# Nine warm-up products on fewer rows, and ten unread operations on GpSimd, in a two-layer attention kernel

## The chip, the cores and the metric

The kernel runs on one core of one Trainium2 chip. The metric is the time of the program on the device in microseconds (us), the median of its runs. The core has a matrix engine (TensorE, PE in the profile, with its weight loads as PEld), VectorE (DVE), ScalarE (ACT), GpSimd (POOL) and SyncE (SP), which here issues most of the transfers. Each engine works through its own queue in order and waits on semaphores for the others.

## The reference

The input x is 2048 tokens of 512 features. Four blocks follow each other, A, B, A, B, each with a layer norm ahead of it and a residual sum behind it:

```
x = x + A(layernorm(x));  x = x + B(layernorm(x));  and both again
A: q, k, v = x@wq, x@wk, x@wv; 32 heads of 16; 4 segments of 512 tokens
   a_dot = softmax(q k^T / 4 + causal mask) v      inside the segment
   a_mem = phi(q) M / (phi(q) z + 1e-6)             memory of the segments before
   out = (g a_mem + (1 - g) a_dot) @ wo,  g = sigmoid(beta)
B: phi(t) = [softmax(t w_phi), softmax(-t w_phi)];  linear attention over all
   2048 tokens: (phi(q) (phi(k)^T v)) / (phi(q) sum phi(k) + 1e-6) @ wo
```

The layer norm needs, for each token, 1/sqrt(variance + 1e-5).

## The kernel before

Tokens lie on 128 partitions, 16 tiles of 128 tokens. A segment is four tiles. The program is written as a list of operations (`Graph.op`) with what each reads and writes. A table named ORDER, a packed text at the end of the file, says in which sequence they are put, which engine takes each (where more than one could), and which buffer each tile of data gets. `place` unpacks it and `emit` derives the waits. So the place of an operation in the source says nothing on when it runs: only the table does.

The parts that matter here lie in the first 25 us:

- `setup` issues the loads of x and of the weights, and makes the constants. `onesb` is a 128x128 tile of ones (L513). The gate is made from beta: an exp on ScalarE, an add (L517) and a reciprocal (L518) on VectorE, and with it each of four slices of the weights WA_v is scaled (L526). The table puts these four scalings on GpSimd; they are called the gates here. The V product of the first segment reads them.
- `ln` is the layer norm of a tile: statistics on VectorE (L570, L571), then for most tiles an add of epsilon (L578) and a power with exponent -1/2 (L580) on GpSimd, each of one column, and then the normalizing on VectorE (L591), which is transposed. The four tiles of the first segment take ScalarE for the root instead (L574, L576).
- `warm` gives PE products of ones with ones that nothing reads, while the first loads are under way. It has 26 units of one 128x512 product each, and after the fourteenth four extra units with small or half-height products. 25 of the 26, with the extras, stand ahead of the first segment's products in PE's queue; the transposes of the first four tiles stand between them.
- `a_proj` makes keys and queries of a segment, four groups of eight heads at a time (L341), evacuates them on ScalarE or VectorE (L359, L360), and multiplies the keys with masks that pick heads (L672). The scores are products of those (L326); their exps are on ScalarE (L351).
- `b_keys` and `kv_add` sum the keys-times-values of block B in the float32 tile KV32 (L890 the first of a layer, L892 the others).

GpSimd's queue at the place of the change is, in the table's order: the add and the power of one tile of the second segment (L578, L580), two gates (L526), two adds, a power, an add, two powers (L578, L580), a memset (L534), two gates, a memset, and further adds, powers and memsets. VectorE's queue there is: statistics of the next tiles, the gate's add and reciprocal between them, then masked key products and the normalizing of the second segment's tiles in alternation.

Of the kernel before, what the change touches and what calls it, by code (L numbers as in the profile page):

```python
# [1108 lines left out]
c-rlH1&|~;lC4}WR%KRIS2Hs+Gcz+YGcz+YGcz+YGcz+YbALs3&(7@b>@C>8|IN-WvQiOJgj~;`yT4SXRYFppR3H^e9HK}90t87VQkhgCRY^5cozx&TNi9;F)FE|AJ  # L1109
yM@EAPq?)(wH<MO-VD-oJ1i}Ni-6d#3ZqZCWKHTh$V(d;v<ZNBb?+S1xaR7h~y?&NC}dMWF>h?VG@s&B>6}-QiLQXrATR#pJXRRNf}ar<RC3bPSTPTBV|b|(waOY@y  # L1110
T<Ngp?ym$pdnQ+#(N26dIjeCAUc|`huh<k;zL^oJ=Pp$qX`z%p^<5Xfln=BNIq!l8W3R*T`M+h|DIhNL2cmTqm>0Tyl@hA!ErHa)b0HZAc%|mo$ZDFo?7zN8uQ>BQs
zogrg(K05XuorcX$F(vNf?{Yfv<g`^`XNeYsYM5Ad)9GaG_B*$SD*$5|K6ZlC02_pB&YjTr3B}>U+I0DPaIMR)bC-cc_5}T|cacKq;oh~4q$wU&KE+n1E3bLGZB_m)
0ydfiDBGiYsqy#j8lE7du{2=ehB+{KMB8v%!$poMy5fB7JNFdoq){zjhmh2~c$X-HVAABb3VFP4=DWoW5g{fpW`9QLRg<vQK*<dqS3R_4IQW};)8Q4lnfr6eSkQRc%
P!-BTLpVUHK_e&v#bFSX#hQ4KRE7*dp%xA%6`&l1077{fN-Dx&r~)-1BZPr?G!tZoWTZIypcYhz=Fk{wzyN3g1ECevhFQ=AhLM&~2WCS(7y`pd4EmLn!=X?Y){`Lmg
|vpYFbX!1jie2<gYp<mYhwf&k%pl=VKnT5BV-I5C6Q=Yh);9CSQrk&U<%BElQ0#=!zq{x@nI5-gUPTT4nP9f4bx#7Y=-$T5B5MfD1q-uauNWQ@f-O>4ERCAN3xS7gy
fJ2Qo|xx3=$T=LP!irASR7W!;?zT9wLyOumx5_8dw9#AUte^ZEy%Wz*yQ5VnGB5p@9&VMugZ96_P>}NCBOp6QqS+5Er^YSBL|VVLOQgy&)Y$gKkg~yF&#WN0-A2*bZ
l4C7gy;(2usD$LS8}PfySxbSP~}Khm}EogRdB@QMDQt!W=9g>|qm#DglB9(q6`5*^M$D|#OK!6tGJF2HvZi7bJhkdgL>U~&<Tk;(Kp$wYh8DYOsWMF!F)^bm;w+ek&
sOEc4^bPzpEn$avYCv8qsLN=P8=Aij#H`<*B;C}iDeAt5?pagqTz{k*+4yMEC0J?+pq9f^WI*QiC5wrjuO;bTVJVj!{C74NH!V`E6&tMk43{z<?m`2Cb+^~>dfvb=Q
uEB0Po9?04VFF!5=hFmq4qZT>)2B2ct%^6`CcL1}=pA?pci|Q!qG{+oxDVCv0VJns=@?oGZ^J`aOefMM^d+4~FOV7Z4O}Fz=p;Iw9;9>WV`}gaT~5=}6?7?GMsv~UP
#ss&SMUPf!YUe;L?kE42~q>w(%du;Jx$)h6Kav+dpJq=QjVwSC)h`i($8>=7NQgjQ$oK0BBkHpBYc1&v>+`<v(vngj+Uh5>0x?=uBNA{!ZlRmTDp!_q+4k*S{k>}ua  # L1120
K2ipvCESnuM;W8)yldl<uHA=|;MVrl6H5(9N_A`Y{mC(lhiN4aWEM0}VonZ|OUFkqZ1wFVQdbI(<!V(5v(teM4{3uk;!Xi(xPWElNW$9PXl9Xd8NqR;K4^6?%c@gFT
oZuF%``GObVdI_QaMRayXQ(FU{{tw~GM@4)CM{EYQ+8*ax2*bo!q9U6xv!jv=>txcO@4O*Svrw`~|nvDK{=2(X|r1$7UT9?LUoCY#M6JrWYim5P&eZY@68H3pr48s(
abSh56L#XLtoQH-k!TGop1L$&Gfj+tr8_`m<47D@~HbOsbfsN@RT!stq2(H9rY%%`8qc|RuGr~6D1l)+La1E};g0L1-;v}4i;jtbqOH<Pb_=wKLS-1mt;%wZ6?Pz<t
8RuXJIv11SK7547a6fLr<M<d;v3uAO@8fRVib>c(Jb=3}HG6<b*+XoNukbatL10br6viMYup>Q*t?)Fi!%lbxlVe+KjO+0%PREG&1u5%{UojFQV=M(r$s%JE?1Hf|D
h|dc$eCa-@F~8;A=rsN!_M>#e#hrH3P<Bx9Eu~b3r&q3uqnpDxEKwiV>}FDkyr%w4!_}h49g<3i0mB3W9Kmn8;-+JvoR={Vll8QwnxLp;sv~jX)r$Cz>XLbZ(=u$&!
VxYEIR9s8(A#Y12?hQEG>({(xQ*0Vg0Z_`dLrBgb7$W9LN%~TX-A$;z%5bm$47tLCdb-RZNe)Far)^G1)m1j<sj!Nn$pcbzq6uNfw?BW>eTHHiQkpLD&w*VQ=h8Gq7
uzj%6b0Sw@zL&A?a~h9tndm=O=NBP<iPVwtfu%ZhE-8Pb-GWdZCuW@cweUd(~xST1bGhO<sAANF7)SZCIgWy7491#@E_%#Qi702W~#Sr^uo6=l6xH<pEUXIWV>R+^P
yWm#|5m-S)&*m|~s6~w8m5EjO4EIXUVHnS~kJe$FWvSDl_o4`h~v+OjR#HO<|>>NAFMzbO~h8<%ESy7zGwz5NP8_U6RvV1H*E5~xN+$;|(&I+)CtPq>Yis39ao0Vj9
SYB3`?Phz}Ubd5MXUEwCwu9|r!1po9DOda<JJ0sB3+w<p!K$zyjPR<gKP$t^v$?Dk8^GqVi|i7+%&xGj>>B&VDzGQ4BCE}+vG43Do6qX7>Z}s0%$~8jtOk3|7O+R`I
{U(Iu*d8xTgVo%#q1`##g?$!tR7p*ma;qSE?dU#vHR>L)7<b^%yQ%boO8inum<b{^Yhp2BYVT%vWDy(d(V9Q5@Gx^`@}AjlzbIi&g!$8tQK3%*08l~1#8S2v30BoOU  # L1130
0YAKpxD)@E{(-!}8QT4G+iD^7K3%&%m3pm^?g>#WV5<JONL{Gx5wkHjm5S@#gG3Ps&@cWIQ2{$RqJMJTi~R6Z0rMDv!pq@RlqIkI$p?6g)Zqz(4ZpJO<Chi}1WWA1}
a*@*2DtugPoi$~-^M%CqsDJUh?D3-Us|FfYza@Eklhufj|6a=a8T&tLJ^yehB8OY;i65--au@-qAlugB}~y1X{8&l~U-Jd1qGTk?jy5pT?!@TR;OZ_Zoswmhr+#6R<
|yc_?*+wt!F8_y=c^X#%UZ_nHC4!k2DD|+*Bq7VPU-F8b*5mrnTJvfSRf{F2>Cyyi|i%FudBfA$5FCvI2q7(1OJM#%*vX~<J^Qc0I0bGi%ybB-0hj1mV2oMALU_OWs
<zu-PJ~4&Q;eL@pZV(yeMlp^L<Ky{oK9^76Q~3x!k5A+Cc|;LSWRg?G3^83y6Vb(15kt%rvqWaOO-$so#YjF!EZ}p+JTaZm;5p?YkwfN^x#cKsM4*T%7K>P7CSS-$^
I3cmpTuYLJaWFsD;M(xVlvMsQ;Pg@p(r2=$_ye%EEg+8u&6Ch^HTB*4-sKRA`x4x6strbSw|L@rR7<Eop0nt<tDz5@8`wjW`2q9<vaLgo=Pkc7x)1lM<f<Y#ZG>nXB
1oc7QT&d=Sf6Tv5Q~i$wX=qSHu%(L?)406p_hAT5*aW<xBVlxs(fahp!gP#6>ApWqFq`<5gr`d5&-3^<;dJKpf}0`8}RRWEIQ#8orXR;D`7szDXSBH+U{}pReXO`5u
`{<yLFNUU{3RRw+b6af>UpR>V<S#Z|pU0+mo@6ZK^ukxrx+>%|eiS*#NWc^TPP^b<Q}1G!%|lqu9Mc|c}S{Y6TZRh^Qj<p6O{R+ZaDBUw%E5XI$MK1d7{5BUSWMO2q
N#eKO??v{t-L77R#Q-|ddSwdu1@l|*gL6sCiY8^i+j`5@NxI7`t$`bOJyuwR~Dq^3gA+O1rvX(r-ON(H2U6vPB#V&D2UXpj^Ww~42kT>N6`B0vbXJtt_M6BoKWDi+E
R21dJ9<g5>6MMx~>9!#1mi#Wy%iHpbJSX$0A2P3stj>tb;<z{<PKZk4k$fV1%E$7Gcq+@wD2k{G(x^lVlvRmUb`eoUQdjv|(NUHWC&fW=Ra_IjWN%qXR+J~@NuE#T5
KQG)g+*g|N;Hwx#UB1lK9|?{X;E3^6xT(5QBB+sc|{G;Np_Z9WFC=A<QDlv5#d*X>V@Pgj0#ZE)GPT?77){vPn8viL_yI?9u^;EG4Wc4sAMXvN~5N$v?{r3CBmr;s<  # L1140
n8=qpIh;n~14i@K5rMEF^A<jH;$+Bf5)@qJXL;3aUrEuzJkTiSweVY$iX;w=$NxAUcTXs<mt<-pTj!i)<s?$`3Mzsx6v|W}<=kDw~TI;t7Asdx++;zGx^qiHoAB=p#
R<^s12hsIsY{0`xGEUG)@=#BkAB)DvAqW6@W(6m3O&QC!p&BSbIplGhR6<PmX6bQOa|6A@btQB>zp-_%g`U8PgQRZ?|9)l?(YMRiQoQpZ(Jl|;Q3C)69!K-E@_R9$s
a6;nl2aaB~6P&ZV6bxYh-1Jp>dLX8r)MML#gd>1X`5AjKi7IoAe@kKON&%|djR;^T{R7o{XT~nphXmwrP7iH94QCd}2WmP#9PcBmN<wNmYELL;WTs2T7kO}1&l}L_M
!_;`SL?xC>RT5c6)l(DHL^Vmh6O&a{RbC~PGt^AAOf6UQ)Dbmbtx~I11@%ExR7ce*HA{u)L29;ItE#E$s)-t`rl`~EmRhL7>f368dZgB<d#b5=tnRCDx|w>Q!s~~sz
FMaqiw)|d*r;BL^=gx9p_;39vWBXplF7|#s%j}8iLSDn{3>1ukVHNa?PYiQUUZP(L_e8aJ{5P=S#?fbQcu+rbzWUo!TPRxr&_8o`n}Tns%oXKs55GdGP;9mtvac;%5
A0eRuw@%5HHj-^-?`oW5jl~O|?<4RA;wwji}$Ku=1_?q<*My^0Ok^YLrql8K9L8FFUH3GEnYN?G%?g)hiK6Mv<}PJrPH8{Z);YJ{=^-NTL1O$Q1I6I;d01NIFRGQ<3
F<l}a8^yVOCoTTPOa<yd)0N0d@VkW=Iy6<bc%{pAc@RR`(;vaOD+m9+AZiYnvEVX~TTr-#e+a=$*HH^?YDnvSZY>w$8j+$3Y@FjC84IYMrfLe|sG^=4ULx6nQH7Fk3
0(lvEgRa@85>-7fRO)b=m^j0}l2FMV(O}1BER1Y;s4wl{3P?=gDR(n-U{aU5copoy6MaR+=bQ+ybXVevSW*u8^)IHTo-AirKt8`o)NBd-N)j*%t)pdJ)M)y%2^k!XG
Z_$->Uv*Jm(zSF~omR)wNpwHeP&d{?WFtLJHqqVmOx;O$)U$MD-BNegt#lQgRF9O&baI_S$Jg`q0^LLR)_wGHJyp-vt#v=$Mz7F^bzeP4Ptyr>Lfu~v)C2S&9Ze3_<
7FnDNH^8#^%1>TZ`IrMUOi7Q(fjmeeMK*p$Mp%lM6T9r^eVYpE|t+`7QI%Ek{R?0Iae>$%k*`9Ro~Fp^mN(Ev^MMXT76s3kazVReNS)KJM|8|OYe}|<q(}%r_?c|Up  # L1150
CY8<a{|(&XLRIN;yr=mJ{S|y+$sRx%5e$Tc6dZ^f{eJ7u5N5VSP)dkvDZ(nNIG}vt(X9SLWC2<WPNI57Q6zd3`~T(8KitSwt7m<MjlcUS`#W^aK4!r!=Wd8S_{l(?!
feQ`ThDMa?3U!#vSPbxzaE^fuXbGLzgq*H85e{Y)>EIrK}NQ;*c?O=^?DywYh*T9d-$GwDn*Gt*==`Asoh+{`kiOlh-7j?zW-L_JAQ)}!?poyBA_SxshBT$j`(bOF=
# [60 lines left out]
```

## Time and profile before

| what | us |
|---|---|
| median of two runs | 493.31 |
| lowest, highest | 492.28, 494.34 |
| the profiled execution | 492.6 |
| its span, first to last instruction | 490.9 |
| PE busy | 460.2 |
| VectorE busy | 436.1 |
| ScalarE busy | 433.9 |
| GpSimd busy | 59.6 |

Busy times overlap; each is the time in which the engine had an instruction running. In the views below, a row of a timeline gives start, length, engine, line and operation, what it wrote and read, and in brackets the idle time ahead of it with what ended it. A row of the groups gives the shape, the count, the busy time and the mean of one in ns. L numbers are lines of the kernel.

### The profile page before, as it was taken

The numbers are of one execution on the slowest core, as the hardware profiler recorded it, in microseconds if no ns is written. First come the engines' busy times: TensorE is split into PE (matmuls) and PEld (weight loads), VectorE is DVE, ScalarE is ACT, GpSimd is POOL, SyncE is SP. The second block draws the span as 40 slices with busy tenths as digits, with TensorE's granted clock in tenths as the row PEclk, the third lists the DMA queues.
The fourth block names the chain that finished last, engine by engine and source line by source line (L and its number), as shares of the span: only waits on it lengthen the run. The fifth ranks groups of instructions, "written<-read, shape, count | busy, mean of one in ns | idle before, by whom it ended". The sixth has DMA issues, their size and how long they took to land.

```text
span 490.9 us, 27235 instructions
## 1 busy us (share of the span) xinstructions
PE 460.2 (94%) x12490; PEld 309.1 (63%) x12490; DVE 436.1 (89%) x1087; ACT 433.9 (88%) x605; POOL 59.6 (12%) x144
## 2 busy tenths in 40 slices
...
POOL 4701031010011001000230240100010010100000
...
DMA packets 89459, 30.50 MB, mean 62 GB/s; under 512 B 76000, under 2 KB 89344, under 8 KB 89344
## 3 DMA queue, kind: packets, MB, share of 16 engines
...
q14 instruction: 17, 0.14, 0.1%
q0 software_dynamic: 64, 0.02, 0.1%
...
## 4 chain that ended last, share of the span: by engine, by line
PE 59%; ACT 25%; DVE 8%; issue 3%; DMA 3%; SPq 1%; POOL 0%; POOLq 0%; DVEq 0%
PE D L341 36%; PE D L326 21%; ACT p L351 16%; ACT pE L351 6%; DMA WA_q<-in_A_wq_dram 2%; DVE pQ L672 1%; ACT pS L351 1%; DVE p L756 1%; DVE pS L925 1%; PE D L854 1%; DVE pK L360 1%; ACT pV L359 1%; DVE p L591 1%; ACT p L359 1%; DVE p L360 1%
## 5 line engine op out<-in xcount | busy, mean ns | idle before, releaser
L351 ACT ACTIVATE p<-D 128x1024 bf16<-128x1024 f32 (+1 forms) x368 | 312.1, 913 | 25.2 <-PE D L326 11.6
L326 PE MATMUL D<-pK,pQ 64*128 64x128 bf16 (+1 forms) x2560 | 115.5, 211 | 4.3 <-ACT p L351 1.4
L326 PEld LDWEIGHTS D<-pK,pQ 64*128 64x128 bf16 x2560 | 80.7, 94 | 43.4 <-ACT p L351 10.9
L351 ACT ACTIVATE pE<-D 128x768 bf16<-128x768 f32 x128 | 102.0, 835 | 4.7 <-PE D L326 3.6
L326 PE MATMUL D<-pV,p 64*128 64x34 bf16 x1536 | 73.4, 176 | 3.9 <-issue 2.9
L326 PE MATMUL D<-pV,pE 64*128 64x34 bf16 x1024 | 75.2, 175 | 0.5 <-ACT pE L351 0.2
L326 PE MATMUL D<-pW,pE 64*128 64x34 bf16 x1024 | 73.0, 175 | 0.1
L326 PE MATMUL D<-pW,p 64*128 64x34 bf16 x1536 | 71.7, 176 | 1.0 <-issue 0.9
L326 PEld LDWEIGHTS D<-pV,p 64*128 64x128 bf16 x1536 | 66.8, 93 | 7.1 <-issue 2.4
L326 PEld LDWEIGHTS D<-pW,p 64*128 64x128 bf16 x1536 | 65.8, 93 | 3.9 <-issue 1.4
L341 PE MATMUL D<-pX,WA_k 64*128 64x512 bf16 x256 | 65.2, 376 | 2.1 <-DMA WA_q<-in_A_wq_dram 1.4
L341 PE MATMUL D<-pX,WA_q 64*128 64x512 bf16 x256 | 65.3, 377 | 0.6 <-issue 0.4
L578 POOL TENSOR_SCALAR rstd<-mv 128x1 f32<-128x1 f32 x60 | 14.9, 265 | 374.0 <-DVE mv L571 367.2
L326 PEld LDWEIGHTS D<-pV,pE 64*128 64x128 bf16 x1024 | 54.8, 93 | 3.1 <-issue 1.5
L326 PEld LDWEIGHTS D<-pW,pE 64*128 64x128 bf16 x1024 | 51.2, 93 | 0.9 <-issue 0.3
L570 DVE BATCH_NORM_STATS2 stats<-X 128x6 f32<-128x512 bf16 x64 | 42.5, 681 | 4.7 <-DMA X<-in_A_x_dram 4.6
L925 DVE TENSOR_REDUCE pS<-p 128x32 f32<-128x512 bf16 x64 | 42.1, 672 | 2.1 <-ACT p L351 1.9
L672 DVE TENSOR_SCALAR pQ<-p,m 128x512 bf16<-128x512 bf16 x128 | 42.6, 355 | 0.6 <-ACT p L359 0.5
L879 DVE TENSOR_TENSOR X<-X,D 128x512 bf16<-128x512 bf16 x48 | 31.1, 682 | 7.3 <-PE D L341 7.1
L580 POOL TENSOR_TENSOR rstd<-rstd,mhalf 128x1 f32<-128x1 f32 x60 | 36.4, 624 | 2.8
L341 PE MATMUL D<-WA_o,p 64*128 64x512 bf16 (+1 forms) x288 | 33.8, 353 | 2.3 <-issue 1.9
L326 PE MATMUL D<-tri,two 64*128 64x256 bf16 x256 | 35.2, 270 | 0.0
...
## 6 DMA issues: line engine op xcount, KB each, us to landing
...
p<-p SPq DMA_TRANSPOSE x76, 3.2
pX<-p SPq DMA_TRANSPOSE x54, 3.2
...
```

The lines of the kernel that those rows point to most:

```text
L326: ins = e.matmul(out_ap, lhsT, rhs, start=st, stop=sp, tile_position=(basep(lhsT), basep(out_ap)))
L341: ins = e.matmul(out_ap, lhsT[64 * hf:64 * hf + 64], rhs[64 * hf:64 * hf + 64], start=k == 0 and i == 0, stop=k == 1 and i == len(lists[hf ...
L351: return self.g.op({"act": (dur, lambda e: e.activation(out_ap(), in_ap(), func, scale=scale))}, reads, writes, opens, label=label)
L359: ch = {"act": (n / 1.2 + 51, lambda e: e.activation(out_ap(), in_ap(), ACT.Copy)), "dve": ((340 if fast else n / 0.96 + 65), lambda e: e. ...
L360: "dve": ((340 if fast else n / 0.96 + 65), lambda e: e.tensor_copy(out_ap(), in_ap()))}
L570: v(lambda e: e.bn_stats(self.stats[:, t, :], self.X[:, t, :]), 602, [R("X", t)], [R("st", t)], label="bn")
L578: v(lambda e: e.tensor_scalar(rs, self.mv[:, t, 1:2], LN_EPS, None, op0=ALU.add), 170, [R("mv", t)], [R("rstd", t)], eng="pool", label="rstd")
L580: v(lambda e: e.tensor_tensor(rs, rs, self.mhalf[:], ALU.pow), 540, [R("rstd", t), R("mhalf")], [R("rstd", t)], eng="pool", label="rstd")
L591: v(lambda e: e.tensor_scalar(xn.t[:], self.X[:, t, :], self.mv[:, t, 0:1], self.rstd[:, t:t + 1], op0=ALU.subtract, op1=ALU.mult), 300, [ ...
L672: fn = lambda e, KM=KM, KT=KT, sl=sl: e.tensor_scalar(KM.t[:, :, sl % 2, :, 64 * (sl // 2):64 * (sl // 2) + 64], KT.t[:].rearrange("p (j h ...
L879: self.v(lambda e, X=X, src=src: e.tensor_tensor(X(), X(), src(), ALU.add), 602, [R("X", t), ps[512 * k]], [R("X", t)], label="res")
L925: fn = lambda e, sgn=sgn, E=E, Z=Z: e.tensor_reduce(Z.t[:, sgn * 32:(sgn + 1) * 32], E.t[:, sgn * 512:(sgn + 1) * 512].rearrange("p (h d) ...
```

## The change

Two operations are added to `setup`: memsets of parts of KV32, used as scratch, on VectorE. Ten operations are added at the end of `build`, all for GpSimd (two rounds of five): a power of 128x64 float32, a power of 128x16, a product of 128x64, a product of a 128x256 bf16 tile with 2.0, and a sum of two such tiles. Nothing reads what they write. All KVacc sums are made to depend on the ten.

Nine of the 26 warm-up units become products on 64 or 32 rows, of 256 columns, two rounds over the row groups; those on 32 rows write into two PSUM buffers. The four extra units shrink.

The table is a new one. Unpacked, it differs from the old one as follows. GpSimd: the ten operations stand together behind the power of the last tile of the second segment (the L580 at 10.97 us in the profile) and ahead of the first two gates; nothing else differs. VectorE: the copy of L535 goes from far behind to third place; the two memsets stand among the first segment's normalizing and evacuations; the gate's add and reciprocal (L517, L518) go behind the next eight statistics operations (five L570, three L571) and the mask sum of L499. ScalarE: the exp of beta goes four places back. PE and SP have the same order. No operation changes its engine. Buffers of PSUM get other numbers, and two buffers of the pool p1 are exchanged in places.

```
+        flat = self.KV32[:].rearrange("p a b -> p (a b)")
+        self.probe, self.z64, self.pb = flat[:, 0:128], flat[:, 0:64], flat[:, 128:384].bitcast(BF16)
+        v(lambda e: e.memset(self.z64[:], 2.0), 70, [], [R("z64")])
+        v(lambda e: e.memset(self.pb[:, 0:256], 2.0), 100, [], [R("pb")])
...
-        D = self.T(self.pD, "S")
+        D, D2 = self.T(self.pD, "S"), self.T(self.pD, "S")
...
-                        ins = e.matmul(D.t[c0:, r0 * 8:r0 * 8 + n], r[:, c0:], ones(r, n), start=True, stop=True, tile_position=(r0, c0))
+                        ins = e.matmul((D if r0 < 64 or rows == 64 else D2).t[c0:, r0 % (rows * 2) * (512 // rows):r0 % (rows * 2) * (512 // rows) + n], r[:, c0:], ones(r, n), start=True, stop=True, tile_position=(r0, c0))
...
+        shapes = {14: 64, 15: 32, 16: 64, 17: 32, 18: 32, 19: 64, 20: 32, 22: 32, 23: 64}
         for k in range(N_WARM):
-            unit(128, 512, 1)
+            if k in shapes:
+                unit(shapes[k], 256, 2)
+            else:
+                unit(128, 512, 1)
             if k == N_WARM // 2:
-                for rows, n, m in ((64, 51, 12), (64, 64, 8), (64, 256, 4), (128, 34, 8)):
+                for rows, n, m in ((64, 51, 1), (64, 64, 1), (64, 256, 2), (128, 34, 1)):
                     unit(rows, n, m)
...
+        pr, one, v = self.probe, self.ones8, self.v
+        for r in range(2):
+            v(lambda e: e.tensor_tensor(pr[:, 64:128], self.z64[:], self.mhalf[:].to_broadcast([128, 64]), ALU.pow), 600, [R("z64"), R("mhalf")], [R("pr")], eng="pool", label="prb")
+            v(lambda e: e.tensor_tensor(pr[:, 64:80], self.z64[:, 0:16], self.mhalf[:].to_broadcast([128, 16]), ALU.pow), 600, [R("z64"), R("mhalf")], [R("pr")], eng="pool", label="prb")
+            v(lambda e: e.tensor_tensor(pr[:, 64:128], self.z64[:], self.z64[:], ALU.mult), 600, [R("z64")], [R("pr")], eng="pool", label="prb")
+            v(lambda e: e.tensor_scalar(self.pb[:, 256:512], self.pb[:, 0:256], 2.0, None, op0=ALU.mult), 600, [R("pb")], [R("pb2")], eng="pool", label="prb")
+            v(lambda e: e.tensor_tensor(self.pb[:, 256:512], self.pb[:, 0:256], self.pb[:, 0:256], ALU.add), 600, [R("pb")], [R("pb2")], eng="pool", label="prb")
+        for o in self.g.ops:
+            if o.label == "KVacc":
+                o.deps.update(self.g.ops[-10:])
```

More of the change, by code (lines that the diff above doesn't have):

```diff
@@ L641, in fn @@
                         r = self.onesb[r0:r0 + rows, :]
-                        ins = e.matmul(D.t[c0:, r0 * 8:r0 * 8 + n], r[:, c0:], ones(r, n), start=True, stop=True, tile_position=(r0, c0))
+                        ins = e.matmul((D if r0 < 64 or rows == 64 else D2).t[c0:, r0 % (rows * 2) * (512 // rows):r0 % (rows * 2) * (512 // rows) + n], r[:, c0:], ones(r, n), start=True, stop=True, tile_position=(r0, c0))
                 return ins
-            self.g.op({"pe": (m * max(n / 2.4 + 2.5, 26.0), fn)}, [self.R("onesb")], [D], label="warm", rows=rows if c0 == 0 else rows * 10)
+            self.g.op({"pe": (m * max(n / 2.4 + 2.5, 26.0), fn)}, [self.R("onesb")], [D, D2] if rows == 32 else [D], label="warm", rows=rows if c0 == 0 else rows * 10)
+        shapes = {14: 64, 15: 32, 16: 64, 17: 32, 18: 32, 19: 64, 20: 32, 22: 32, 23: 64}
         for k in range(N_WARM):
-            unit(128, 512, 1)
+            if k in shapes:
+                unit(shapes[k], 256, 2)
+            else:
+                unit(128, 512, 1)
             if k == N_WARM // 2:
-                for rows, n, m in ((64, 51, 12), (64, 64, 8), (64, 256, 4), (128, 34, 8)):
+                for rows, n, m in ((64, 51, 1), (64, 64, 1), (64, 256, 2), (128, 34, 1)):
                     unit(rows, n, m)
@@ L1108 @@
 ORDER = """
[L1109 to L1152, printed above, removed]
@@ L1153 @@
-Cyw(LxOOwmwHgEJ>{Z5b7@AX&xL4VUz^f+C}bTXYyVYA+pH|0!8lhBkfc})_t!6Y(?O;XdrbToNPAJf+iFau2~J;apOL(O;nQGe1u^k-ec5L3xiG?h&moy}A+Uo@CO
-ri&@7+nB+ot7&V>X==*r?53*eVbJt6&CGDq-h?sDjW*UWBg|^E#)Oz|rkZJIwwg#LiV17Nn{CDzZlnn?KBG)^Q^V9W{mn45)ATdl%`P*_j4-3kNHfOlHjB+h<2QTE6
-0^xnH#5vy6KJ-Z=w_YSVV0X1W`!AR#+fZ<ya{J&naHMrscjmXI;N3nY=TW))5HXsdS-%&Y9^XVX0n-LBABTrqKRpunOJ7FnPZxo`ev`$XXcvCW}XRWmzwZ)nVDuH*o
-bz%xnLHUi)N)+WiFZP=8Cy#;+fbczBy?2n?vS+IcyS`2j+-5Y95*w=9qbD9+@ZRmAPSVnak#}Ic`pvljf8;ZO)iGCfMFJam-Wm+?+M%%z5+1JTr04Z4<_RHid174Qs
@@ L1157 @@
-!cBKE8KZi?Dswuhy*r|o5XTeMfrHFM9rHs8#B^TRL;mRN3u&2K-Lx8|dHXFi$tCcqZ3J}Ye(t87>6x7u18WCN|S1#KZ)(w4GOY;haeMzT?D3ERzfx6y2A8{MY2S!@}
-b)n>3UY)o6$mb0;Jc^lhSuyJff8`t);@of^@*Cw^`Y&M(BX0*v|P20!zw*zb~JJ43LRcuw8z*e@|?I4@U*0zIfLOa9`wJmKE+sZbzEA2=-%#O0dZ6Z6)uCn889oyO_
-wry+*o5N<d&Fl!<+^)83?L0f*uCpoaOq<HCv9oMlo71+nE$l|S$>y@_?FPHWZnj(PHoMQ}w)<^0Tis5u3+zO@(2lmV?HHTdrnPfyUc24yusiK8yW8%ud+h;x(AKb%>
->@kXrm=HvKAXq3v+eC++rf6U_3SxY-yX5&Z6`a~Ubj>1Vtd0LvPbPPd)!{I7i}YZ(@wXy>=L`w-nPqa13T4rwvFv2o6b(N%WOlt!p^WK>`8md-mz!wX?xaQwpZ*`d(
@@ L1173 @@
-zi4oznnEtE~m%{k-^8pC6A;zP@*>&0O<(j8r#AS}l;6N{;P7~2jLQT6F$}1Z{pWA0D2>8XN<HWi!2Ze^h<ro-O9ByWyEBPR5T(P<-9&Jn#ZyqJVUbXs&%Rg7UZe9pg
-)Ef{20|S`T16REg142Iw{Ep9Hmj%Irs4Njdff^YPt!M4>69SAAieRt$z=?}O76t?T#7gi5xo{K564xdKs71dModBw7prY`90K_d(O#
+c-rlH1C%YxvTa7BGrM~=wr$(CZQHhO+qP}nwr$(qKdbjX=j?m#x$k29_x~7gyjs1gDzh>pXUvG0RkcPZAQebOQi;SSio_>CD5*@UkgB8_sZMH;nxqz~P3n-kq#mhH8
+jyyh5ot`Ckfx*=X--;@$RrAhN-~o;BnF8|G$90uAeI;+i9cZ^Ea4<KDMYf6!XyvLN=lNvBpb;`ijcUZ6v<DrlcFRMDNV|d0wf11M#_?cBqwP}a*<Y~I4MV3lQ!fziA
+P?L#H2h)LLQQ<<TiOkqGB|1jocxz@g>PXB9T|51erlbk(p#PnMIb8F=RTKPbQLw_K|&TpV+7NnSE|w*q8Q|O-hoHG$b{-ORkf9<T05;UXy6}gxnyr$vkqO%q8Q<SaO
@@ new lines @@
+r}A#F)t(vLKQ<}jGFBgf!4v?nuR7KF!<WFQ$t;^0%#f%GRG$pF%ubS3FYDw2|9BGEA|iHqsTDslo=lTC0EHbVgMBZ1@rc|&fIXJi>U0!Lvv8Be;C31k6TLt>G&Bpzl
+YF>oR2LMD+2xQKKnE6EDdjf{ke@Rp2%Nzee^k&@65N`ZiV0PvnnCOybvvV=&OLMU`13W8xM@sa&xJqaP}$N{pK>>~*K;S1RS8zC!9CB+~cOe1^9N0I~lAq0v;cGyCe
+!B*0fl!4_?7PgVnV4xQX!opAlszEtu1P4iVXbeT61Pq39v=%)?sz63yP@4`R6`?$Y1r8Np7^wt9peodYOb`a*V`j(#$w>+7gW6C7T0j%12?L=e41(5B2WCT47*1M2U
+6=#)VJM6sG4UHIPlrK0*g%5uD`^AmU^Hwbn@C$|4;5$#)}awG5{AKDFa~zRQ8E^ek;oVh5@1dk2P0rOOoh2{3Z}sXI1Te40ZfMRFa-|4K}ZODU<OQwEwBLQ!(IpvCF
@@ new lines @@
+uu}f&@Sn`kj0xeh>&2K9OA{5u|{`kOmgR640;^7C{n73b8N>h9i}s1B55JU@NSFw6GSELj>3c+u<;DgmKsjVnaj-i$M?$BS9R92FV~Qq=YWe8PY*-hzDJv8^nbuu!B
+T~K9C-wLw6`edq71x9#_Ch*a2r@6`X<9&>vgk3ET+-@FWh!Vb}^k;W}5OhhRN?Mxbr5FO;TrX+MY$RcQw32?<FII0voq0`!N?<UCvi0ujkl=mnW@00fasaGXrR6C^Y
+C!Kv66cauTb6c3Y_u$@$*`7jGM!@+ojG{>x%3tM0+$c_atC+5fQ*aHLT0elQT+7k~V(q2gE6X=ISa5xUcouoI8!Vx$c>(P-|5XWF@s83ImSa2C;;VXCwZ{Ru1#w#!l
+bHj9;fO%jMUWIFr7p}t|oP&Gu228}oxBwI4TwI7R@EIn;YV;=Df|vLl@4_><2e%<Hrp5d40IJi6kOI@;SgcI%z#~|KlW-}%!ufcS%*3~FiM+<iI0FyiJbZ$F^f0c#4
@@ new lines @@
+7d`P;d0E4FQ5ipg|Fcyyo1#khD0Ez$VpO@w!=J_7tfIQ@D%;2pda8A?n6mW<7e29$M6dr$HK^H5k&k7oHG0lpWq`D#X?vfb6`G5kEO5z9>Jry2G5|OYthnmxE?FvHY
+|>1=yv=D*{~v(z#W(rH{eDriOFy$?!ryD8B=0qq__pk(m)zS&*51-k0JB}e#Bs^={tOnmr&6!cp1Oq4Sa()@fv=|w|EP`;dKm0!_bUa48zj!bT@9rws;$>;03IT7co
+EVr3K(B-oY!_0QXUjNw69ggxc5;t79!Jg9HVBreA0Sx}ENz4QV5qh~CAxEHO=msj&_=r!}z#KEQ`~50fKc3tAT&;eC9B^)Mcj7{nANp($xHnwkc)kMt9rLPOY88ipC
+vIE_xHhpELQbUyXNrE~#ZMgwpKT}geoh&IO3SQh;;DQ!#xu_bMSi|KN@kRGM0XmYlM0y{=0&=d^WMmmvhqO0jzx`q~lbu<;7OefI@v_6)@G#HUS##wYW-AQ-RIdn5^
@@ new lines @@
+j~#Feol867Jer*Dr;q7zdVp@FC+HKJn%$?Z=mWZkZlg)rA$pMRrfJwinv6Z7ZRl(IhPI`YHKnI%baIk*!c(+0Jww;i&h#uzLEF(LbOSv{XV6IWD`l(;{YE2G&IC)zQ
+n4sBD(y<+&}eiBeM%)$>?M6hU(unoGd`zX@GT|m1szSt(06ng9Z9=l8rqRIqj70G8lA?V@o88VnMGvp>38~phGS7!BzB(0XBTKxHi8bPmW`#F85WavqaCOp8%HnFOE
+fJ_KyT7cG#0%@yVC?LI*Z0)upV?1i_Ln{%`6T}$6~T{)W_1Y{&WBhWWDHRnvkWZgIFSVo8F=Q=qNgfUZH*IUFy%S(rYvW?M*Y%!7LU#Pr|bf>;g%`rm&7IF+0T~upw
++JJI#i&fpjo!Psh_fv>Rq**J*l|fn{Qu*-RRn29t#J9?e9Lu%j$9ZOyXKHY^)$%g&N^Y#a+<H)s}ij^v{`>3Ei#wr3+)XO^G#WFuJ@){AAQxoB3Jhvua@XaQP~7G<4
@@ new lines @@
+SSJsUcW4&2-mX-Bj*;sK_hLvRHSRdAp^=19p2DXtEqSIJmT7+h2IoNczg>7XM*i1Hz4QHd+L^hh8V`tc8HiMmI=h-nfh83k_*>QG=6{C~bHg=e8XE|9emY)@1<ymf)
+hvj7@SV2~Z6=t(oaXOpLVWrqymX8%-d)QvKkL_YR*a`NK?PR+d<@=fDj2r%lU0?^;MRt&#WK|h(<ki>!R+d#@^H^y%kj-b8*kyKwU1itUb@rWAWKUToR)<w*gg;{oS
+Y1|wRc2M#b5@VlWG~o4_L$vZU)fFegneU+*kZPX-D0=dQg(;cXRFvUc9-2_%h`SQfW2at`|;PzpK~6-C0G0<YsfybK>mh(VsF_y)`-1lADE9{CW3!qpV<|XimzrXSO
+Zpz)n;qhTDFd@WKCFOww^U*sd+ON#6x%(9?Zk?a6Ao9%fs_@JOfY9GxFvv7LUMV^GrM<PskJV%sdN^!{hPyyaoHflkt`;IZwnR@yI+bkHX{gBs?mQ#-sDBycJ8z6Yv
@@ new lines @@
+;3B~QUW@=v@5kID1$qC6kZ&kOQmye2QsYw_B=3NOI3@$5Vo&%tx^LcB09!b|XyJSWe?tMXF3JTJ{F@Ynneug0tMGQ1+M%**jgyexmq>+`z29<Re2@P@o4&nn;XR=g2
+!%$xA0ycuuKTkzJr9nU5|^Dq1x@6NyS_PhuG&a+D*a>zEk18>Va@=ko5=)=d0z8nM!Dwqf-CW)S$i||5-38EK|ETV|Xq92!{H;*79im0M9@6WsNiDHVFDhBXqLWzM~
+i*CFtAIpbwBm6~x7{rJ0!F(7W$F1;*seCRE6dC14kx6b6<N0ttfsf$x_(VR9kL2_DbiRN`646CwIZezIGsJWeLu?Z<#Vj#fWRcs&BtA!s;&a79K2OXSGx$uNOD+~UW
+p0^Aj^=(MNW>CLL~JpOFXChPY`&OJ=5u&nxj^KTOZY-Dh3A*4L;<--6qJQzMiDGlh?OEl)RAX+X?d216=6hT5l5^Nt3_d1R~C_F<T-wWZ{o$|X1<>v;Kk(@ewpv%JN
@@ new lines @@
+Xr!S}YY8`9U66BoWKRE`EV$65IGzzMb#jNkuZTn_uF|MH&%L#20BrW|2h{l_^9zahf0FOZi2)j4O4QuMx||C8<>vd5<sWRb@SSo^Ry!Wde~<oZx%-eV$ch6D#;yzKX
+Bphxuy0SsdXvd2aQ9ui>}&UYT0uQESCMd55P_DMcc2n;W%G#8p<sQ+-52l}Ke54P;-DUStp(#8JLQtQUuPS=mqY7rSIbc|bOjDb;RyP-ayFL@Jd{ot9_hKyhDIlRHF
+XSzYcFCFD9jSPT-6_(Q%`)R4Qx1G!)Bk%#3WnOVhGN90jiQe;sHR0I`Kl@h^fJwGOn^JDUaJSoe`lJdB`%1eu?V!x;<ughApwmiwph!Ax{RuI+1ZgE#$miOcpxkucT
+x8y_lNS>AFWGOjRY~bZ(Pgzk^66M8SaX=gw`@}VO<KgPIB<g~^Bd^NyGOq%aPeoB@#T9Wv926%-W${=(mA&K>c~v}<6=YO}s-pB$i4|4;Dv8P=BB{vg8b2pG$+F^<I
```

47 lines of the change are left out of this document (35 added, 12 removed).

## The prediction

> **What bounds the kernel now.** I read the page first, then the chain that ended last in order of time, then the timelines of GpSimd (POOL) and VectorE (DVE) over the first 25 us, and last the groups of GpSimd by form.
>
> The page says that three engines share the bound and that one does not:
>
> ```profile
> span 490.9 us, 27235 instructions
> ...
> PE 460.2 (94%) x12490; PEld 309.1 (63%) x12490; DVE 436.1 (89%) x1087; ACT 433.9 (88%) x605; POOL 59.6 (12%) x144
> ...
> POOL 4701031010011001000230240100010010100000
> ```
>
> PE, VectorE and ScalarE are each near 90% busy, so a delay of all three is hardly won back later. GpSimd is 12% busy, but its second slice (12.3 to 24.5 us) shows a 7. That is where the change puts its ten operations: between the root of the second segment's last tile and the first gate.
>
> The chain shows what carries the path there:
>
> ```profile
> 3.30 8.56 DMA WA_q<-in_A_wq_dram
> 11.95 2.78 PE D L341 x24
> 14.75 0.60 ACT p L359
> 15.46 0.35 DVE pQ L672
> 15.81 0.32 DVE p L591
> 16.22 0.50 DVE pQ L672 x2
> 16.72 0.32 DVE p L591
> 17.05 2.52 DVE pQ L672 x3
> ```
>
> The first products wait for the weights until 11.95. From 15.46 to 24.24 the chain lies on VectorE, and L591, the normalizing of a tile, is a link of it. It reads the tile's rstd, made on GpSimd. The first number is the start, the second the length. Next GpSimd itself:
>
> ```profile
> 10.36 0.23 POOL L578 TENSOR_SCALAR rstd<-mv 128x1 f32<-128x1 f32 x1 [6.04 <-DVE gt L517]
> 10.54 0.30 POOL L534 MEMSET pE<- 128x256 bf16 x1
> 10.79 0.09 POOL L493 MEMSET mhalf<- 128x1 f32 x1
> 10.97 0.57 POOL L580 TENSOR_TENSOR rstd<-rstd,mhalf 128x1 f32<-128x1 f32 x1
> 11.51 2.06 POOL L526 TENSOR_TENSOR WA_v<-WA_v,gt 128x512 bf16<-128x512 bf16 x2
> 14.47 0.39 POOL L578 TENSOR_SCALAR rstd<-mv 128x1 f32<-128x1 f32 x2 [0.89 <-DVE mv L571]
> 14.82 0.57 POOL L580 TENSOR_TENSOR rstd<-rstd,mhalf 128x1 f32<-128x1 f32 x1
> ...
> 17.27 2.15 POOL L526 TENSOR_TENSOR WA_v<-WA_v,gt 128x512 bf16<-128x512 bf16 x2
> ```
>
> The new operations go in at 11.51. Behind them stand the gates (4 in all), the adds at 14.47 and the root at 14.82, which the L591 at 16.72 reads. That root ends at 15.39, and L591 is taken by VectorE at 16.64 (its row in VectorE's timeline, 16.72 in the chain): 1.25 us of slack, and 0.89 us of idle time on GpSimd ahead of it. GpSimd has only 2.1 us to give.
>
> The groups by form give the prices:
>
> ```profile
> L580 POOL TENSOR_TENSOR rstd<-rstd,mhalf 128x1 f32<-128x1 f32 x60 | 36.4, 624 | 2.8
> ...
> L526 POOL TENSOR_TENSOR WA_v<-WA_v,gt 128x512 bf16<-128x512 bf16 x4 | 4.2, 1072 | 0.0
> ...
> L508 POOL TENSOR_SCALAR_AFFINE_SELECT p<-p 128x128 bf16<-128x128 bf16 x1 | 0.3, 292 | 0.0
> ...
> L497 POOL TENSOR_SCALAR_AFFINE_SELECT H<-H 128x8 f32<-128x8 f32 x1 | 0.2, 192 | 0.1
> ```
>
> **The change, part by part.** *The ten GpSimd operations, d us in all.* Plain ones: two inputs cost 1.07 us for 512 columns, 2.1 ns a column; one input costs (292 - 192)/120 = 0.83 ns a column on 0.19 us. The median add of one column is 0.222 us (the view of L578 alone; that of L580 gives 0.567 for the power). So the 64-column product is 0.222 + 64 x 0.0021 = 0.36, the 256-column scalar product 0.19 + 0.21 = 0.40, the 256-column sum between 0.535 (half a gate) and 0.76 (with a start of 0.222), taken as 0.65. Each twice: 2.8 us.
>
> The powers are the open cost: the trace has powers of one column only, 0.567 us, 0.345 above the add. Low end, a column costs what it costs in a gate: 0.567 + 63 x 0.0021 = 0.70 and 0.567 + 15 x 0.0021 = 0.60, twice 2.6 us; d = 5.4. High end, every column costs the whole 0.345: 22.3 and 5.74, twice 56.1 us; d = 58.9. No gain is possible, since no operation leaves GpSimd. The power's own row is nearer in kind than the gate's, so the column must cost a good part of 0.345; but a single column overstates it, as it does for the select (0.192 for 8 columns, 0.292 for 128). I take a quarter, 0.085 us a column, an estimate that lets some four columns be under way at once: 0.567 + 5.36 = 5.92 and 0.567 + 1.28 = 1.84, twice 15.5; d = 18.3 us.
>
> By the Trainium skill, GPSIMD Engine Reference, section 3.1 (Elementwise), a two-input elementwise operation runs at about 2.6 cycles an element at 1.2 GHz, 2.2 ns. The gates agree (2.1 ns). Were a power one of these, the time would be that of the first rival below; no run here shows it.
>
> *What waits.* The gates start at 11.51 + d. Without the 0.89 us of idle time the root is ready 2.06 + 0.92 us later, at 14.49 + d (0.92 is 14.47 to 15.39). VectorE takes L591 at 16.64 today, so it is late by d - 2.1: 3.3, 16.2 or 56.8 us. VectorE works in order: behind L591 stand the other masked-key products (L672) of the first head group, for which PE's score products wait, and for those ScalarE's exps. All three stop. The later work of GpSimd is not late beyond that: the next root is 1.8 us behind and is read 2.9 us later today (19.49), and the last two gates would end 4.3 us behind L591 where the V product starts 4.7 us behind it (21.30).
>
> *The gate's factor.* The add and the reciprocal of the gate (L517, L518) move behind eight statistics operations and the mask sum (L499) on VectorE, from a reciprocal ended at 10.9 to one at about 15.5 (the last of these ends at 14.96). The first gate needs it. It costs nothing while the ten operations hold GpSimd to 16.9 at least; without that cover the first gate would be 3.9 us late and L591 some 1.9 us.
>
> *Warm products on PE.* Four extra units shrink. Today 24 products of 51 columns, 16 of 64, 8 of 256 and 8 of 34 take 5.8 to about 7.05; after it 2, 2, 4 and 1 take about 0.35: 0.9 us less. Nine of the later units are cut into 64 or 32 rows. On 64 rows, two halves run side by side (the L341 pairs of 64x512 start within 0.02 us and follow each 0.215 us), so a unit stays at 0.215. On 32 rows no row shows it: 0.215 when four run abreast, 0.86 one by one. I take the first, being nearest to the 64-row pairs; five such units: 0 to 3.2 us. A change of row height: the 64-row load came after 0.42 us of idle time, the 128-row load after 0.21, against 0.28 between loads of one height; so 0 to 0.42 for each of some eleven changes, taken as 0.1. In all -0.9 + 1.1, near nothing; ends -0.9 and +6.9. It is covered twice: the first products wait for WA_q until 11.95 with the transposed inputs ready at 10.65 (1.3 us), and past that a late PE runs beside GpSimd's 16 us. Without the second cover the high end would cost 5.6 us.
>
> The Trainium skill's TensorEngine Tiling (Array Packing), section Tiling Modes, states that changing the tiling mode drains TensorE. The 0.42 us above may be such a drain; with it on every change, the unit sum above stays under the same cover and the forecast is the same.
>
> *PE's clock.* While VectorE waits, PE stands for some 16 us. At the start the 512-column products came every 0.43 us until 4.4, for 3.3 us, and then every 0.215. Coming back so would lose 1.65 us, of which the 1.09 us that PE idles ahead of the V product may cover part: between 0 and 3, taken as 1.0.
>
> *The rest.* Two memsets on VectorE (0.17 us for 128x128 at L513) lie ahead of waits. The 128x64 copy of L535 (0.14 us at 155.7) moves to VectorE's first 3 us, idle for the first X: -0.14. The added wait of all KVacc sums on the ten operations ends by 71 us at the worst; the first sum (L890) is at 119.7. The PSUM and p1 buffers are mostly renamed: 0, with 1 us either way.
>
> Sum, against the profiled execution (492.6 us, span 490.9 and 1.7 around it): 492.6 + 16.2 + 1.0 - 0.2 = **509.6 us**. That execution is 0.7 under the median of the runs, 493.31.
>
> **The rivals.** *A power's column is cheap* (under 0.04 us): 492.6 + 3.3 - 0.2 = 495.7 at the low end, up to about 503. For it: the gate's 2.1 ns. Against it: 0.345 us for a single column is a lot of computing. Two per cent (9.9 us on 493.3, about what a measurement of this kernel can tell from no change) is reached near 0.04 us a column: d = 2.8 + 2.27 + 156 x 0.04 = 11.3, so 9.2 late and 1.0 for the clock, less 0.2.
>
> *Every column costs its full 0.345*: 492.6 + 56.8 + 1 - 0.2 = 550; from 0.2 us a column (528) on I count it here. For it: the only power row there is. Against it: a quotient from one column holds the start of the operation too.
>
> *Not slower: the GpSimd work is hidden.* GpSimd idles 21.4 us ahead of 45.15, and if the new operations ran there, the lateness would be 0 and only the 0.2 us of VectorE and a shorter warm-up would show: 492.4, at best 491.5. It decides when d is under 2.1 us or when nothing reads a root behind them. Against it: d is 5.4 even at the low end, and L591 reads such a root at 16.64.
>
> *The warm-up fails*: late transposes and a half clock at 11.95. The slice at 455 to 465 shows a granted 0.50 with PE 3.50 of 5 us busy, so a lull is enough. It would add 5.6 us to the first Kev but runs beside GpSimd's delay, so alone it gives 498; it decides only if the powers are cheap.
>
> **How the numbers follow.** Forecast (0.04 to 0.2 us a column) 0.43; cheap powers 0.27, the failed warm-up within it; full price 0.25; hidden 0.05. Slower by over 2%: 0.43 + 0.25 = 0.68. Within 2%: 0.27 + 0.04 = 0.31. Faster: 0.01, since nothing here removes 10 us. The range starts at the low end of the cheap case, 495.7, and goes to 540 (0.28 us a column), leaving out the hidden case and half of the full price.
>
> **What would show it.** Right: on GpSimd the 64-column powers take near 5.9 us and the 16-column ones 1.8; the ten end near 30 us; L591 waits for rstd, for about 16 us; from then on everything is shifted by one amount up to the end; the KVacc sums wait for none of it. The forecast is wrong in its size if the powers lie elsewhere, and wrong in its mechanism if the shift is much smaller than the ten operations less 2.1 us, or if a lull of PE around 9 to 12 us is what the chain shows.

## The result, and the profile after

The changed kernel takes 521.01 us in the median of two runs (519.57 and 522.45), the kernel before 493.31. The ratio is 1.0562, with a 95% interval of 1.0404 to 1.0719: slower by some 28 us, as forecast in sign and inside the range, and 11 us above the predicted 509.6. The ratios here and below, with their intervals, are formed from the single undisturbed runs of both kernels, so they can differ by some 0.2% from the quotient of the medians given. The profiled execution took 522.45 us, 29.85 more than that of before.

The page of the changed kernel, the same lines as before:

```profile
span 520.7 us, 27247 instructions
...
PE 462.8 (89%) x12490; PEld 311.2 (60%) x12490; DVE 436.3 (84%) x1089; ACT 434.1 (83%) x605; POOL 89.2 (17%) x154
...
POOL 3999110310000201010023023010101011100000
```

Busy time of PE, VectorE and ScalarE is as before within 3 us; only the span grew, by 29.8, and GpSimd's busy time by 29.6. The three engines did the same work and stood still in between. GpSimd has its 9s in the second to fourth slice, 13 to 52 us. The chain of waits, in order of time (start, length, what), says who held them:

```profile
13.12 10.52 POOL KV L1090
23.71 2.91 POOL KV L1091
...
28.53 10.51 POOL KV L1090
39.12 2.91 POOL KV L1091
...
43.92 2.02 POOL WA_v L530 x2
...
46.31 0.54 POOL rstd L584
```

L1090 is the power of 64 columns and L1091 that of 16, twice each. The gates (L530) follow at 43.9 and the root (L584) at 46.3. VectorE's timeline has the wait itself; first the same operation in the kernel before, then the changed kernel:

```profile
16.64 0.41 DVE L591 TENSOR_SCALAR p<-X,mv,rstd 128x512 bf16<-128x512 bf16 x1
```

```profile
17.62 0.58 DVE L680 TENSOR_SCALAR pQ<-p,m 128x512 bf16<-128x512 bf16 x2
46.88 0.41 DVE L595 TENSOR_SCALAR p<-X,mv,rstd 128x512 bf16<-128x512 bf16 x1 [28.68 <-POOL rstd L584]
```

L595 is the L591 of before, and L680 its L672: lines moved down by the added code. The normalizing started at 16.64 before and at 46.88 now, 30.24 later. After it the shift stays: 30.6 us at the exps, whose rows in the chain of the kernel before and of the changed one are

```profile
26.64 2.85 ACT p L351 x3
```

```profile
57.24 2.85 ACT p L351 x3
```

then 30.5 at the first KVacc sum (150.2 against 119.7; the ten were long over by then) and 29.8 at the end. The groups of GpSimd by form give the prices:

```profile
L1090 POOL TENSOR_TENSOR KV<-KV,mhalf 128x64 f32<-128x64 f32 x2 | 21.1, 10540 | 0.0
L1091 POOL TENSOR_TENSOR KV<-KV,mhalf 128x16 f32<-128x16 f32 x2 | 5.8, 2904 | 0.2
L1093 POOL TENSOR_SCALAR KV<-KV 128x256 bf16<-128x256 bf16 x2 | 1.8, 880 | 0.0
L1094 POOL TENSOR_TENSOR KV<-KV 128x256 bf16<-128x256 bf16 x2 | 1.2, 612 | 0.2
```

Behind the first bar stand the busy time in us and the mean of one in ns, behind the second the idle time ahead of them. The sum of the ten, with the products of 64 columns at 0.292 us and the gaps, is 13.10 to 43.88: 30.8 us, where the forecast had 18.3.

### The profile page after: what moved, and what is told of

Same layout as the page of the kernel before. It is cut to its first block, busy times and chain, and to the rows that moved or that the text cites. A ratio compares the mean times of both kernels' runs of the same rounds, so it can differ in the third digit from the quotient of the medians.

```text
span 520.7 us, 27247 instructions
## 1 busy us (share of the span) xinstructions
PE 462.8 (89%) x12490; PEld 311.2 (60%) x12490; DVE 436.3 (84%) x1089; ACT 434.1 (83%) x605; POOL 89.2 (17%) x154
## 3 DMA queue, kind: packets, MB, share of 16 engines
q1 hardware_dynamic: 88992, 28.46, 30.5%
## 4 chain that ended last, share of the span: by engine, by line
PE 53%; ACT 26%; DVE 7%; POOL 7%; DMA 3%; issue 2%; SPq 1%; POOLq 0%; DVEq 0%
PE D L341 32%; PE D L326 20%; ACT p L351 17%; ACT pE L351 6%; POOL KV L1090 4%; DMA X<-in_A_x_dram 2%; POOL KV L1091 1%; ACT pS L351 1%; DMA p<-p 1%; DMA pX<-p 1%; DVE pS L933 1%; DVE stats L574 1%; ACT pV L359 1%; DVE p L595 0%; DVE p L764 0%
## 5 line engine op out<-in xcount | busy, mean ns | idle before, releaser
L326 PE MATMUL D<-pK,pQ 64*128 64x128 bf16 (+1 forms) x2560 | 116.4, 212 | 33.3 <-DVE pQ L680 28.3
L341 PE MATMUL D<-pX,WA_k 64*128 64x512 bf16 x256 | 66.8, 384 | 2.6 <-DMA WA_q<-in_A_wq_dram 2.1
L341 PE MATMUL D<-pX,WA_q 64*128 64x512 bf16 x256 | 66.9, 385 | 1.0 <-issue 1.0
L595 DVE TENSOR_SCALAR p<-X,mv,rstd 128x512 bf16<-128x512 bf16 x48 | 18.8, 396 | 30.7 <-POOL rstd L584 30.6
L680 DVE TENSOR_SCALAR pQ<-p,m 128x512 bf16<-128x512 bf16 x128 | 42.1, 352 | 0.1
L584 POOL TENSOR_TENSOR rstd<-rstd,mhalf 128x1 f32<-128x1 f32 x60 | 36.1, 622 | 2.8
L341 PE MATMUL D<-WB_k,pX 64*128 64x512 bf16 (+1 forms) x288 | 34.3, 353 | 1.7 <-ACT pE L351 0.7
```

Of the source, the lines that this page charges most:

```text
L326: ins = e.matmul(out_ap, lhsT, rhs, start=st, stop=sp, tile_position=(basep(lhsT), basep(out_ap)))
L341: ins = e.matmul(out_ap, lhsT[64 * hf:64 * hf + 64], rhs[64 * hf:64 * hf + 64], start=k == 0 and i == 0, stop=k == 1 and i == len(lists[hf ...
L584: v(lambda e: e.tensor_tensor(rs, rs, self.mhalf[:], ALU.pow), 540, [R("rstd", t), R("mhalf")], [R("rstd", t)], eng="pool", label="rstd")
L595: v(lambda e: e.tensor_scalar(xn.t[:], self.X[:, t, :], self.mv[:, t, 0:1], self.rstd[:, t:t + 1], op0=ALU.subtract, op1=ALU.mult), 300, [ ...
L680: fn = lambda e, KM=KM, KT=KT, sl=sl: e.tensor_scalar(KM.t[:, :, sl % 2, :, 64 * (sl // 2):64 * (sl // 2) + 64], KT.t[:].rearrange("p (j h ...
```

## The experiments

The theory is that all of the loss is GpSimd's queue: the ten operations stand ahead of a root that VectorE reads in order, so the loss is their length less the 2.1 us that GpSimd had to give. Rivals: the new warm-up products or the new order carry part of it; powers on GpSimd hold up VectorE wherever they run; the lull has a price of its own through PE's clock; the loads, which landed later in the profiled run, belong to the change. The first four kernels ran on one chip, where the kernel before took 495.94 us in the median, the others on another, where it took 492.38; each is compared with the kernel before on its own chip.

**The kernel before once more** (no edit).

> The kernel before, unchanged, for a second trace. In the profiled run of the changed kernel the weights that the first products wait for landed at 13.5 us where they landed at 11.95 before, and all that follows, the first of the ten operations too, began some 1.6 us later. If that is chance, this run may show anything from 11.9 to 13.5; if it belongs to the change, this run and every kernel with the old warm-up shows 11.9 and every kernel with the new one 13.5. Time 492 to 495.

One run: 496.23 us. The first product starts at 12.25 us. Taken over all the traces it starts at 11.95, 12.25, 11.98, 11.99, 12.19 and 12.99 in kernels with the old warm-up, at 13.50, 12.21, 13.13, 11.71 and 11.97 in those with the new one. Both kinds have early and late starts, so the late start is a matter of the single execution. Of the 29.85 us between the two profiled executions, 1.6 are this; 28.3 are left, near the 27.7 between the medians.

**Without the ten.**

```
 def place(self, pools, table):
     ...
-        self.order = order
+        kill = {o for o in order if o.label == "prb"}
+        for o in order:
+            o.deps -= kill
+        self.order = [o for o in order if o not in kill]
```

> The changed kernel without its ten GpSimd operations; nothing else is left out. Queue theory (all of the loss is the ten operations ahead of a root that is read): only the later gate factor is left, the first gate starts when the reciprocal ends, at about 15.5 us instead of 11.5, L591 is 1.9 us late: 494 to 495.5. Warm-up rival (the new products delay the first keys or leave PE at half clock): 498 or more, with the loss ahead of the first L591. Reordering rival (the new buffer numbers cost later): 495 to 500 with the loss spread over the span.

497.89 us, 1.0018 of the kernel before (0.9983 to 1.0053), so between 0.8 us faster and 2.6 slower. Warm-up, order and buffers together cost nothing that the times can tell from zero. The gate factor can be seen in the trace, though; GpSimd first, then VectorE:

```profile
15.87 2.12 POOL L533 TENSOR_TENSOR WA_v<-WA_v,gt 128x512 bf16<-128x512 bf16 x2 [4.34 <-DVE gt L525]
```

```profile
15.91 1.16 DVE L598 TENSOR_SCALAR p<-X,mv,rstd 128x512 bf16<-128x512 bf16 x1
...
19.03 0.41 DVE L598 TENSOR_SCALAR p<-X,mv,rstd 128x512 bf16<-128x512 bf16 x1 [0.63 <-POOL rstd L587]
```

The first gate waits 4.34 us for the reciprocal (L525 here), and the normalizing that was at 16.64 is at 19.03, 2.4 us late, of which 0.26 is the later first product (12.21). The forecast had 1.9 for this once the ten are gone.

**The ten alone.** To the kernel before, the two memsets and the ten operations are added at the changed kernel's places; warm-up and order stay.

```
+        order.insert(order.index(ops[238]) + 1, sets[1])
+        order.insert(order.index(ops[69]) + 1, sets[0])
+        at = order.index(pool[1]) + 1          # behind the first root of GpSimd
+        order[at:at] = ten
```

> The kernel before with the ten operations and their two memsets alone, at the same place of the GpSimd queue; old warm-up, old order elsewhere. Queue theory: L591 is late by 30.8 - 2.1 = 28.7 us: 521 to 522.5, as the changed kernel. If the new warm-up or the new order carries part of the loss, this is faster than the changed kernel by that part: 515 to 519.

524.30 us, a ratio of 1.0565 (1.0526 to 1.0604), the changed kernel's 1.0562. With the first product at 12.99 the normalizing starts at 46.82, behind 29.06 us of waiting for the root. The ten alone reproduce the whole loss.

**The ten where GpSimd is idle.** The same ten, in the kernel before, in two groups of five, behind the roots that end at 294 and at 317 us; their scratch is the same KV32, free there, and the memsets go to GpSimd.

```
+        for k, x in ((95, pick("prc")), (91, pick("prs") + pick("prb"))):
+            at = order.index(pool[k]) + 1       # pool: the adds and roots on GpSimd
+            order[at:at] = x
```

> The kernel before with the same ten operations moved to where GpSimd has nothing to do: five ahead of the adds at 315 us (20.7 us idle) and five ahead of those at 342 (25.8 us idle), 15.4 us each. Queue theory: hidden, 492.5 to 494.5. Port rival (a power on GpSimd keeps VectorE from its fast operations wherever it runs): VectorE's L672 and L591 rows of 0.35 us grow in these stretches, and the time by 3 to 10 us: 496 to 503.

496.06 us, a ratio of 1.0004 (0.9972 to 1.0037): 30 us of GpSimd work at no measurable cost. Nor do the powers hold up VectorE. Its masked-key products from 294 to 343 us, kernel before and then this one, by form:

```profile
L672 DVE TENSOR_SCALAR pQ<-p,m 128x512 bf16<-128x512 bf16 x18 | 5.7, 337 | 0.0
```

```profile
L682 DVE TENSOR_SCALAR pQ<-p,m 128x512 bf16<-128x512 bf16 x16 | 5.1, 335 | 0.0
```

The mean of one is 337 ns without the powers and 335 with them, where eleven of the sixteen ran beside a power. The port rival falls.

**Fewer columns.** In the changed kernel, the 64-column powers become 16-column ones.

```
-            v(lambda e: e.tensor_tensor(pr[:, 64:128], self.z64[:], self.mhalf[:].to_broadcast([128, 64]), ALU.pow), ...
+            v(lambda e: e.tensor_tensor(pr[:, 64:80], self.z64[:, 0:16], self.mhalf[:].to_broadcast([128, 16]), ALU.pow), ...
```

> The changed kernel with the two 64-column powers cut to 16 columns, so four powers of 16. The trace has 10.53 us for 64 columns and 2.90 for 16, so the ten take 30.8 - 15.3 = 15.5 us. Queue theory: the loss shrinks by the same 15.3 us: 505 to 507. If the loss were partly a fixed price of the lull (PE's clock, buffers), it would shrink by less: 508 to 512.

507.12 us, a ratio of 1.0299 (1.0249 to 1.0350). The ten run from 12.72 to 28.26, 15.5 us, and the normalizing starts at

```profile
31.26 0.41 DVE L595 TENSOR_SCALAR p<-X,mv,rstd 128x512 bf16<-128x512 bf16 x1 [13.43 <-POOL rstd L584]
```

that is 15.6 us earlier than in the changed kernel, with its first product 0.4 earlier: 15.2 for 15.3 of GpSimd work. Up to the normalizing, the queue passes its length on one to one. By the times the loss is 14.7 us, 13 less than the changed kernel's 27.7; the intervals, some 2.5 and 7.8 us either way, cannot tell this from 15.3.

**Without the powers.** The changed kernel with the four powers dropped in the same way as the ten above.

> The changed kernel without its four powers; the six plain operations stay, some 3.6 us by the trace (0.29, 0.88 and 0.61, twice). Queue theory: the six end at about the time at which the gate's reciprocal is ready, so this is like the kernel without the ten or up to 1 us slower: 494 to 496. If plain operations too cost more than their rows, 497 or more.

493.55 us, a ratio of 1.0039 (1.0007 to 1.0072), 0.3 to 3.5 us slower. The six plain operations end at 14.9, the first gate still waits 0.57 us for the reciprocal, and the exps that were at 26.64 are at 28.52, 1.9 late: the gate factor again. Four powers carry all but this.

**PE kept busy through the lull.**

```
-                unit(128, 512, 1)
+                unit(128, 512, 121 if k == N_WARM - 1 else 1)
```

> The changed kernel with the last warm-up unit repeated 121 times, so that PE has 26 us of products nobody reads in the stretch in which it stood still. Clock theory: in the changed kernel the products behind the stretch came every 0.43 us until 52 us, then every 0.215, and between L591 and the exps at 57 us the shift grew from 30.24 to 30.60: this run keeps 0.215 from the start and is 0.3 to 0.5 us faster than the changed kernel, 520 to 521. By the forecast's term it would be 1.0 us faster. If the slow products were hidden altogether: no difference.

521.84 us, a ratio of 1.0597 (1.0550 to 1.0645): against the changed kernel's ratio nothing can be told by time. The traces tell it. The first products behind the lull, in the changed kernel and then in this one:

```profile
48.01 0.63 PE L341 MATMUL D<-pX,WA_k 64*128 64x512 bf16 x1
...
48.44 0.63 PE L341 MATMUL D<-pX,WA_k 64*128 64x512 bf16 x1
```

```profile
46.29 0.38 PE L341 MATMUL D<-pX,WA_k 64*128 64x512 bf16 x1
...
46.51 0.38 PE L341 MATMUL D<-pX,WA_k 64*128 64x512 bf16 x1
```

They follow each other by 0.43 us against 0.22. From the normalizing to the first long run of exps it is 10.36 us in the changed kernel (57.24 - 46.88) and 9.88 here (55.21 - 45.33): at this place the half clock costs 0.48 us. The ten alone, with the same lull, has 10.40 (57.22 - 46.82); without the ten, or without the powers, it is 9.88 again (28.91 - 19.03 and 28.52 - 18.64). In the kernel before it is 10.00.

**The ten behind the start phase.** As the ten alone, but behind the last root of the first 25 us: `pool[1]` becomes `pool[11]`.

> The kernel before with the ten operations behind the gates and the last root of the start phase (the L580 at 23.1 us) instead of ahead of the gates. GpSimd is then idle for 21.4 us before its next adds at 45.15. Queue theory: only the excess over that shows, 30.8 - 21.4 = 9.4 us, less the slack of whoever reads those roots (0 to 2 us): 500.5 to 503. If moving them out of the start phase were enough: 493 to 495. If the place made no difference: 521.

501.36 us, a ratio of 1.0180 (1.0137 to 1.0223), 6.7 to 11 us slower. GpSimd's next adds start at 55.04 instead of 45.15, 9.9 late, and the normalizing that reads the next root, at 47.87 before, waits:

```profile
56.46 0.41 DVE L603 TENSOR_SCALAR p<-X,mv,rstd 128x512 bf16<-128x512 bf16 x1 [8.76 <-POOL rstd L592]
```

It is 8.6 us late, 1.3 less than GpSimd. The same ten cost 28, 9 or 0 us, by place alone.

**Prices.** In GpSimd's idle time of the kernel before, behind the same two roots as above: 11 plain operations of several widths, then seven powers.

```
+        for n in (1, 2, 4, 8, 16, 32, 64):
+            pw(n)                               # 128 x n float32, exponent -1/2
```

> The kernel before with a row of prices measured in GpSimd's idle time ahead of the adds at 315 and 342 us: products of 1, 16 and 64 columns, scalar products and sums of 2, 64, 128 and 256 bf16 columns, powers of 1, 2, 4, 8, 16, 32 and 64 columns. From the two rows of the changed kernel a power is 0.36 + 0.159 us a column: 0.52, 0.68, 1.0, 1.6, 2.9, 5.4, 10.5 us, on one line. If several columns were under way at once from some width on, the wide ones would lie under the line drawn through the narrow ones. The forecast had 0.085 a column: 0.65, 0.82, 1.16, 1.84, 3.2, 5.9. The time stays within 2 us of the kernel before, since the 23 us fit into the idle 25.8.

One run, 492.98 us. GpSimd by form, five of the seven powers (mean of one in ns behind the comma):

```profile
L1101 POOL TENSOR_TENSOR KV<-KV,mhalf 128x64 f32<-128x64 f32 x1 | 10.5, 10520 | 0.1
L1101 POOL TENSOR_TENSOR KV<-KV,mhalf 128x32 f32<-128x32 f32 x1 | 5.7, 5699 | 0.1
L1101 POOL TENSOR_TENSOR KV<-KV,mhalf 128x16 f32<-128x16 f32 x1 | 2.9, 2893 | 0.1
...
L1101 POOL TENSOR_TENSOR KV<-KV,mhalf 128x4 f32<-128x4 f32 x1 | 1.1, 1082 | 0.1
...
L1101 POOL TENSOR_TENSOR KV<-KV,mhalf 128x1 f32<-128x1 f32 x1 | 0.7, 674 | 0.0
```

From 4 columns to 64 it is (10.52 - 1.08)/60 = 0.157 us a column, from 1 to 4 0.136, from 16 to 32 0.175: one line within a tenth, with no gain for wide ones. A product of one column took 0.233 us. Of the 0.345 us between a one-column power and an add, 0.157, nearly half, is paid again by every further column, and the rest once.

## Why the prediction came out as it did

- **Where the change acts.** That the ten stand ahead of the gates and of the root that L591 reads held as forecast: ten alone 1.0565, idle 1.0004.
- **The rule for the loss, d - 2.1.** It held to 0.1 us: d is 30.8, which gives 28.7; L591 was 30.24 late, of which 1.6 are the later loads.
- **The size of d.** This is the step that was off. The powers' term was 15.5 us and measured 26.9, since a column costs 0.157 to 0.159 us and not the assumed 0.085. That is 11.4 of the 12.5 us by which d was too small. The plain operations took 3.6 instead of 2.8, the scalar product of 256 columns alone 0.88 instead of 0.40; 0.3 are gaps. The bounds from both sides, 5.4 and 58.9, held it. The choice of a quarter between them had no row behind it, so that the range held the result is owed to its width. Two rows of different widths were what was missing.
- **The rule of the Trainium skill** (GPSIMD Engine Reference, section 3.1 (Elementwise): about 2.6 cycles an element) is near the 256-column sums, 0.61 us or 2.4 ns a column with the start in it. It does not carry over to powers: at the 1.2 GHz that this page of the Trainium skill gives, 0.157 us is some 190 cycles, an estimate. There the measurement decides, and the rival of the cheap column (495.7) fell.
- **PE's clock.** Put at 1.0; up to the exps it cost 0.48, and nothing in the run with 16-column powers, whose step from the normalizing to the exps is 9.88 as in the filled run. There the granted clock stayed at 0.50 until 35.4, 3.4 us behind the first product, and VectorE hid it; in the changed kernel it stayed at 0.50 until 53.0, 5.4 us behind the first product, and PE became the link of the chain. The lull was 13.0 us there and 28.3 here, where the forecast had some 16. With PE filled, the V product waited 0.46 us for the last gates, which the forecast had as covered; in the changed kernel PE came later and did not wait.
- **The warm-up.** Put near nothing, and measured so together with the order (0.9 us, between -0.8 and 2.6). The step behind it can be read in the changed kernel's weight loads: two 32-row units in a row took 0.54 us and a single one 0.33, so a unit takes 0.21, four row groups abreast, and a change of row height some 0.12 where 0.1 was taken.
- **The gate's factor.** Free behind the ten, as said. Without them it came out at 2.1 us for L591 where 1.9 was said.
- **Chances.** Slower by over 2% had 0.68. The measured column price lies in the likeliest case, 0.04 to 0.2 us.

What stays open is why the loads land up to 1.8 us apart from run to run, and which waits give back the 0.8 us between the shift of 30.6 at 57 us and of 29.8 at the end.
